# Gated linear attention and an MLP mixer on one core: batch 0's decay logits loaded in runs of four tokens, small work of batch 0 rearranged

## The chip, the cores and the metric

The kernel runs on one core of a Trainium2 chip. The metric is device time in microseconds (us) for one execution. A profiled execution gives a trace; its span is the time from the first to the last instruction, and some time lies around it.

## The reference

Four inputs q, k, v and f_logit, each [4 batches, 8 heads, 768 tokens, 48], float32, and the weights of a mixer. Cut to what is computed:

```python
f = 1.0 / (1.0 + np.exp(-f_logit))
state = np.zeros((B, H, D, D))
for t in range(S):
    state = f[:, :, t, :, None] * state + einsum('bhd,bhe->bhde', k[:, :, t], v[:, :, t])
    y[:, :, t] = einsum('bhd,bhde->bhe', q[:, :, t], state)
x = y.transpose(0, 2, 1, 3).reshape(B, S, 384)
h = np.maximum(x.transpose(0, 2, 1) @ w_tok1, 0.0) @ w_tok2      # tokens: 768 -> 256 -> 768
u = x + h.transpose(0, 2, 1)
out = u + np.maximum(u @ w_ch1, 0.0) @ w_ch2                     # channels: 384 -> 1536 -> 384
```

## The kernel before

A batch's 768 tokens are six chunks of 128, one token to a partition. A decay f becomes L = ln(1 + exp(-f_logit)); the running sum of L inside a chunk is a matmul with a triangle of ones. With G = exp(-sum) and Gi = exp(sum), a chunk is an ordinary masked product: q*G and k*Gi are turned by TensorE, multiplied with each other ("scores"), masked (AmT) and multiplied with v; a 48 x 48 state for each head carries the rest to the next chunk.

For one chunk the steps are, with their lines:

- f, k, q and v are loaded (`load`, L368). f of batch 0 goes through SP's DMA queue, one transfer of 128 x 8 x 48 float32 for each chunk, in runs of 48 floats (192 bytes). k, q and v go through POOL's queue, which casts them to bf16. A `mark` (L364) is a one-element memset by POOL into the place where a chunk's f will land: the transfer on SP waits for it, so it starts when POOL has come so far.
- `gates` (L449): Exp and Ln on ScalarE (L456, L457). L is float32; its upper two bytes are read as a bf16 (`Lhi`), and VectorE subtracts them from L for a second bf16 (`Llo`, L462). For batch 0 this split is made for chunks 0 to 2 only (`SPLIT = 3`).
- `sums_and_turns` (L505): the sums on TensorE. Split chunks take eight one-column matmuls for the sum at the chunk's end (L527, L528) and two of 384 columns with `tri_bf` (L529, L530); chunks 3 to 5 of batch 0 do both in float32 (L518, L520). ScalarE makes G, Gi and `glast` (L540, L542, L545), VectorE multiplies them on q and k (`qk`, L550), TensorE turns them (L560), VectorE or ScalarE copies the result to `qkT`.
- `attention` (L464): scores (L479, on 48 rows from partition 0 or 64) and the chunk's own part of the state (L495).
- `rest` (L578): AmT (L597, or for two halves of batch 0 a copy on ScalarE L589 and a mask on POOL L592), `tsum` and `state` (L606, L609, L611), its copies to `state_bd`, the output matmuls (L628, L635), and copies of the output from PSUM as `x_bf` (bf16) and `x_nat` (float32). For chunks 3 to 5 of batch 0 the output stays in its PSUM bank (`KEPT = 3`), where tok2 adds to it.

`mixer` (L660) then runs tok1 (L665, relu to `h1T`), tok2 (L677), the sum u (L687, and `u_bf`), transposes of u (L699, `uT` L704), ch1 (L715, relu to `zT`, in two halves of the tokens, `th`) and ch2 (L734, final sum L740, store L744).

The order is not written out. Every step is an `Op` with the engines that may do it, a rank, and what it needs and makes. `Plan.order` (L179) places all of them by a table of costs; where it may choose it takes the earliest start, shifted by a lag, and then the lowest rank. `SHIFTS` (L20) replaces rank and lag of 382 numbered steps. The result is a fixed program for each engine, in which every engine works strictly in its order and waits on semaphores. The planner hands out the eight PSUM banks too, and where it expects TensorE to be idle early in the run it puts in matmuls on a constant tile (`idle`, L781, the fills), into bank 7, which is kept for them until 25.5 us of its own clock.

On POOL the order of DMA issues is the order in which `load` and `load_w` are called (L394 to L428): batch 0's chunks, tok1's, tok2's and the two halves of ch1's weights, f and two chunks of batch 1, ch2's weights, and so on. POOL also makes the constants `tri` (a triangle) and `ident` (an identity) at the start.

Of the kernel before, what the change touches and what calls it, by code (L numbers as in the profile page):

```python
# [20 lines left out]
    (5,-30,1300), (13,0,1400), (15,0,800), (46,200,3000), (73,30,1000), (78,90,900), (80,120,900),  # L21
    (90,300,1600), (98,300,1300), (137,30,1100), (141,30,1500), (143,30,1200), (145,60,800), (150,60,800),
    (151,-457,1500), (152,60,800), (154,60,800), (157,60,800), (158,60,1000), (159,60,1100), (161,60,1400),
    (163,60,1800), (164,60,1800), (166,90,1600), (168,90,1000), (170,90,400), (174,90,800), (175,-217,1100),
    (179,90,500), (180,90,800), (182,90,600), (184,90,1400), (186,90,1000), (187,90,2500), (192,120,400),
    (194,120,1600), (195,120,800), (198,120,1600), (210,150,1500), (211,150,1000), (213,150,1100),
    (215,150,1700), (216,150,1400), (218,150,1600), (220,150,1000), (221,150,500), (222,150,800), (224,842,0),
    (225,270,900), (226,270,1600), (229,270,1600), (232,275,200), (233,275,600), (241,281,1500),
    (247,283,2000), (248,283,2700), (250,284,2300), (252,284,2800), (253,285,3000), (255,285,3100),
    (256,290,2500), (258,291,2300), (260,292,2000), (261,292,2600), (263,293,3200), (265,294,3100),  # L30
    (267,295,3000), (269,300,1600), (270,703,400), (271,305,700), (273,310,1900), (274,-287,0), (275,315,2800),
    (276,806,0), (278,-324,0), (279,325,2200), (281,330,700), (283,335,400), (286,457,0), (288,459,0),
    (292,360,200), (294,1119,400), (295,365,1000), (296,370,200), (299,375,100), (300,55,0), (301,380,500),
    (304,390,100), (306,-148,0), (307,395,800), (309,400,300), (310,727,400), (311,405,2100), (312,410,300),
    (313,410,300), (314,415,400), (315,415,2300), (321,267,0), (322,405,0), (324,460,500), (326,540,0),
    (331,540,100), (337,393,0), (341,620,300), (342,633,100), (350,330,100), (355,225,0), (356,410,200),
    (358,490,800), (359,490,900), (360,490,1100), (361,490,1000), (362,490,1200), (365,300,900),
    (366,300,3400), (367,300,1100), (371,370,300), (387,360,700), (389,360,800), (390,360,400), (392,360,2400),
    (393,360,1800), (395,425,0), (397,360,900), (398,346,2400), (399,360,1400), (401,360,1600), (402,360,1300),
    (404,440,900), (407,440,1300), (408,54,0), (410,440,300), (411,490,1000), (414,440,600), (416,440,300),  # L40
    (421,440,400), (425,440,600), (428,440,100), (430,440,300), (431,440,300), (438,440,900), (440,520,600),
    (441,568,800), (442,530,800), (443,520,500), (451,520,400), (458,408,0), (461,520,300), (463,520,700),
    (466,520,300), (471,399,0), (473,380,0), (477,38,0), (478,676,0), (498,584,500), (508,-265,0),
    (510,-105,0), (512,194,0), (513,585,1700), (516,765,0), (520,422,0), (521,711,1400), (524,544,0),
    (525,725,1400), (534,914,0), (535,760,1300), (536,855,0), (538,717,0), (540,843,0), (541,781,1300),
    (544,290,0), (551,816,1700), (552,699,0), (554,528,0), (556,506,0), (558,702,0), (560,1007,0), (562,998,0),
    (569,1029,0), (570,905,1300), (572,1308,0), (573,1122,0), (574,980,600), (577,998,0), (580,995,1800),
    (589,1115,300), (593,590,200), (597,590,1300), (598,467,0), (601,703,0), (602,690,300), (603,690,300),
    (604,790,200), (605,790,600), (607,790,400), (608,790,1100), (615,620,400), (623,727,0), (630,620,900),
    (633,730,0), (634,620,1500), (636,620,600), (637,620,1200), (638,620,1200), (640,620,2700), (642,740,0),  # L50
    (645,720,400), (646,720,200), (647,720,600), (648,730,600), (649,720,1100), (651,720,400), (657,662,0),
    (658,518,0), (667,720,3200), (671,720,700), (672,739,0), (673,720,1400), (674,720,2100), (679,720,1200),
    (680,720,900), (681,854,0), (683,820,400), (685,820,300), (687,820,1600), (691,820,1000), (693,820,400),
    (698,820,1800), (700,820,1600), (701,820,1600), (702,820,3200), (708,820,1200), (715,574,0), (721,631,0),
    (728,970,1700), (731,971,2100), (734,972,1600), (737,973,1600), (739,974,1200), (740,974,3000),
    (743,975,1400), (746,971,600), (751,1222,800), (753,974,400), (754,890,0), (760,1094,200), (762,1101,400),
    (766,1253,0), (770,1179,0), (771,1129,300), (772,275,0), (774,1358,0), (784,1178,700), (785,1178,2500),
# [21 lines left out]
    (1077,1914,4400),  # L79
)  # L80
KEPT = 3
SPLIT = 3


class Op:
# [200 lines left out]
def kernel(  # L286
# [12 lines left out]
    nc = tc.nc  # L299
# [515 lines left out]
```

## Time and profile before

| | us |
|---|---|
| median of 3 runs | 183.9 |
| lowest, highest | 183.29, 185.35 |
| the profiled execution | 183.67 |
| its span | 181.9 |
| mean granted TensorE clock | 0.991 |
| busy: TensorE, VectorE, ScalarE, POOL | 171.4, 128.2, 111.4, 86.1 |
| fills (27 records of 30 instructions) | 9.6, the last at 27.5 |

Fills count as busy time of TensorE. A matmul's record runs from its start to a modelled end, and several are in flight, so the sum of records says less than the distance of starts. The page's slices are 4.55 us long. In a row of a timeline the columns are start, duration of the group, engine, line and operation, output and inputs, count, and in brackets the idle time of the engine just before it and what ended it. In the chain they are start, duration and what. In a table of stretches they are the stretch and its length, then for each engine its busy time and number of instructions, then the granted clock and the DMA figures.

When batch 0's f arrives is read from its six transfers: issued at 0.8, 1.4, 3.3, 7.4, 10.0 and 12.7 us, the first used at 3.42, the second at 5.83, the last four landing 4.4, 4.7, 5.8 and 6.5 us after their issue.

### The profile page before, as it was taken

Reading aid. Unit: us, or ns where it says so; the run is one execution under the profiler, and the core shown is the slowest. Engines: PE = TensorE matmul, PEld = TensorE weight load, DVE = VectorE, ACT = ScalarE, POOL = GpSimd, SP = SyncE. Lnnn points to the kernel's source line nnn. Section 1 sums busy time; section 2 is a strip of 40 time slices with the busy share of each in tenths; the row PEclk is TensorE's granted clock in tenths of the full one; section 3 lists DMA queues with packets and bytes.
Section 4 is the critical chain, followed back from the end, with each engine's and each line's share of the span. In section 5 each row is a group of like instructions: output and inputs, shape, how many; then the busy total and the mean of one; then the engine's idle time right before and its main releaser. Section 6 shows DMA issues by size and latency. Waiting matters only on the chain.

```text
span 181.9 us, 4513 instructions
## 1 busy us (share of the span) xinstructions
PE 171.4 (94%) x1807; PEld 111.7 (61%) x1810; DVE 128.2 (70%) x279; ACT 111.4 (61%) x268; POOL 86.1 (47%) x114
## 2 busy tenths in 40 slices
PE   6759998899999998999999999999999999999992
PEld 2337755566767765676766676776666566666662
DVE  7558996849788986997868849798976736344123
ACT  5558884679995469986789646648754402564100
POOL 7999628947579918979656812221201001000000
PEclk9987999999999999999999999999999999999999
DMA  7999996999999999999999991110000004110033
GB/s 101 131 168 156 140 204 87 228 185 160 197 143 156 273 166 147 97 122 68 225 152 116 128 165 43 44 46 4 0 4 0 2 4 173 43 43 0 4 130 130
DMA packets 88820, 19.95 MB, mean 110 GB/s; under 512 B 81536, under 2 KB 87984, under 8 KB 88800
## 3 DMA queue, kind: packets, MB, share of 16 engines
q0 software_dynamic: 78960, 13.77, 94.8%
q1 hardware_dynamic: 9840, 5.90, 11.1%
q8 instruction: 14, 0.23, 0.5%
q14 instruction: 6, 0.05, 0.1%
HBM read 25.17 MB, written 4.72 MB: 164 GB/s over the span
## 4 chain that ended last, share of the span: by engine, by line
PE 52%; DMA 22%; POOL 12%; ACT 6%; DVE 3%; issue 2%; DVEq 0%; POOLq 0%; ACTq 0%
PE ps L734 19%; PE ps L715 13%; DMA f_sb<-in_f_logit_dram 11%; DMA w_ch<-in_moe_w_ch_dram 8%; POOL qk_sb L379 6%; PE ps L560 3%; PE ps L677 3%; DMA qk_sb<-in_q_dram 3%; POOL v_sb L379 2%; PE ps L665 2%; PE ps L479 2%; POOL f_sb L379 1%; PE ps L518 1%; PE ps L635 1%; PE ps L781 1%
## 5 line engine op out<-in xcount | busy, mean ns | idle before, releaser
L734 PE MATMUL ps<-w_ch,zT 128*128 128x384 bf16 (+2 forms) x300 | 53.0, 319 | 0.0
L715 PE MATMUL ps<-uT,w_ch 128*128 128x384 bf16 x288 | 51.6, 326 | 0.0
L445 ACT ACTIVATE zT<-ps 128x384 bf16<-128x384 f32 x72 | 34.7, 493 | 20.4 <-PE ps L715 19.7
L734 PEld LDWEIGHTS <-zT 128*128 128x128 bf16 x300 | 28.0, 98 | 16.6
L715 PEld LDWEIGHTS <-w_ch 128*128 128x128 bf16 x288 | 27.1, 98 | 16.5
L597 DVE TENSOR_TENSOR AmT<-ps,tri_bf 128x512 bf16<-128x512 f32 x46 | 30.3, 683 | 5.1 <-PE ps L479 4.8
L740 DVE TENSOR_TENSOR x_nat<-x_nat,ps 128x384 f32<-128x384 f32 (+2 forms) x25 | 13.3, 535 | 13.8 <-PE ps L734 13.4
L379 POOL DMA_DIRECT2D qk_sb<-in_q_dram x19 | 18.6, 977 | 4.8 <-DMA w_ch<-in_moe_w_ch_dram 3.1
L379 POOL DMA_DIRECT2D qk_sb<-in_k_dram x19 | 18.8, 987 | 3.8 <-DMA f_sb<-in_f_logit_dram 2.7
L440 POOL CAST state_bd<-state 48x192 bf16<-48x192 f32 x20 | 7.5, 374 | 24.7 <-DVE state L611 11.3
L379 POOL DMA_DIRECT2D v_sb<-in_v_dram x19 | 18.7, 985 | 0.9 <-issue 0.9
L560 PE MATMUL ps<-ident,qk 128*128 128x128 bf16 x192 | 15.3, 221 | 2.4 <-DVE qk L550 2.2
L447 DVE TENSOR_SCALAR zT<-ps 128x384 bf16<-128x384 f32 x24 | 12.7, 552 | 6.8 <-PE ps L715 6.7
L550 DVE TENSOR_TENSOR qk<-qk_sb,GG 128x768 bf16<-128x768 bf16 (+1 forms) x30 | 14.1, 482 | 4.2 <-DMA qk_sb<-in_q_dram 3.1
L560 PEld LDWEIGHTS <-qk 128*128 128x128 bf16 x192 | 12.1, 99 | 6.3 <-DVE qk L550 4.4
L456 ACT ACTIVATE f_sb<-f_sb 128x384 f32<-128x384 f32 x24 | 12.1, 523 | 5.2 <-DMA f_sb<-in_f_logit_dram 5.2
L540 ACT ACTIVATE GG<-ps 128x384 bf16<-128x384 f32 x24 | 11.7, 488 | 5.4 <-PE ps L530 4.9
L462 POOL TENSOR_TENSOR Llo<-L 128x384 bf16<-128x384 f32 x11 | 9.0, 826 | 12.5 <-ACT L L457 12.4
L436 ACT ACTIVATE u_bf<-x_nat 128x384 bf16<-128x384 f32 x17 | 8.1, 521 | 10.7 <-DVE x_nat L687 10.7
L573 DVE COPY qkT<-ps 128x1024 bf16<-128x1024 bf16 x18 | 12.2, 684 | 1.0 <-PE ps L560 0.5
L457 ACT ACTIVATE L<-f_sb 128x384 f32<-128x384 f32 x24 | 12.3, 519 | 0.3
L687 DVE TENSOR_TENSOR x_nat<-x_nat,ps 128x384 f32<-128x384 f32 x21 | 10.4, 549 | 2.9 <-PE ps L677 2.9
(70 smaller groups left out, 256.4 us busy)
## 6 DMA issues: line engine op xcount, KB each, us to landing
out_dram<-x_nat SPq DMA_DIRECT2D x23, 192.0 KB, 1.9
f_sb<-in_f_logit_dram POOLq DMA_DIRECT2D x3, 1152.0 KB, 10.7
qk_sb<-in_k_dram POOLq DMA_DIRECT2D x18, 96.0 KB, 6.8
qk_sb<-in_q_dram POOLq DMA_DIRECT2D x18, 96.0 KB, 6.1
v_sb<-in_v_dram POOLq DMA_DIRECT2D x18, 96.0 KB, 6.1
f_sb<-in_f_logit_dram SPq DMA_DIRECT2D x6, 192.0 KB, 4.6
w_ch<-in_moe_w_ch_dram POOLq DMA_DIRECT2D x2, 576.0 KB, 8.0
w_ch<-in_moe_w_ch_dram POOLq DMA_DIRECT2D x1, 1152.0 KB, 13.9
```

Of the source, the lines that this page charges most:

```text
L379: lambda eng=eng, into=into, of=of: eng.dma_start(out=into, in_=of),
L445: nc.scalar.activation(out_, in_, AF.Relu, bias=0.0, scale=1.0)
L447: nc.vector.tensor_scalar(out_, in_, 0.0, None, ALU.max)
L456: add(ACT, r, lambda: nc.scalar.activation(fb, fb, AF.Exp, bias=0.0, scale=-1.0), make=[key], kind=el)
L457: add(ACT, r, lambda: nc.scalar.activation(full, fb, AF.Ln, bias=1.0, scale=1.0), need=[key], make=[whole], kind=el)
L550: add(DVE, r, lambda n=n: nc.vector.tensor_tensor(qk[i][:, n, :, 0:D], qk_sb[nb][:, n, :, c, :], GG[i][:, n], ALU.mult), need=[(x, nb, c) ...
L560: nc.tensor.transpose(to[:, o + hp, :], blk(src)[:, hp, :], ident)
L573: add(DVE, r, lambda: nc.vector.tensor_copy(qkT[i], banks[p_t[0].at].bitcast(BF16).rearrange("p (n t) -> p n t", t=C)), make=[("qkT", i, 0 ...
L597: add(DVE, r, lambda half=half, made=made: nc.vector.tensor_tensor(half, made(), tb4, ALU.mult), need=["tri_bf"], make=[("AmT", i, p)], ba ...
L715: nc.tensor.matmul(banks[pm.at][:, 0:384], lhsT=w[:, kt, c0:c0 + 128], rhs=uT[:, kt, cols], start=(kt == 0), stop=(kt == 2))
L734: nc.tensor.matmul(banks[pm.at][:, 0:n1 - n0], lhsT=zT[:, kt, tt * 128:(tt + 1) * 128], rhs=w_ch2[:, kt, n0:n1], start=(kt == 0), stop=(kt ...
L740: add(DVE, rank("ch2", tt), lambda un=un, pm=pm, n=n1 - n0: nc.vector.tensor_tensor(un, un, banks[pm.at][:, 0:n], ALU.add), make=[("x_nat" ...
```

## The change

Chunks 2 to 5 of batch 0 (`WIDE`) get their f in two transfers (one for even, one for odd heads) in which partition p holds tokens 4p to 4p+3 of those 512, so that a run is 4 x 48 floats (768 bytes). Both are issued right behind the f of chunks 0 and 1; no mark is left. Exp, Ln and the split are done on half of all this at a time (`wide_gates`). Token 4p+j then lies in row p, part j, and chunk 2+g lies in the row quarter from 32g: its sum is made of matmuls on 32 rows each, for the four parts j, for the upper and the lower bf16 (`wide_sums`). The triangle's rows in that order (`tri4`) are made on TensorE with a picking matrix (`wide_constants`); both borrow space in `zT`. The four chunks' sums leave in four banks at once, the sums at the chunks' ends in one piece (`glast_w`). G and Gi get five buffers instead of two.

```diff
-SPLIT = 3
+WIDE = range(2, 6)
...
+    def load_wide(n):
+        hs = slice(n, H, 2)
+        of = f_logit[0, hs, 2 * C:6 * C].rearrange("h (p j) d -> p h (j d)", j=4)
+        into = f_sb[0][:, hs, 2:6, :].rearrange("p h j d -> p h (j d)")
+        add(SP, -8.0, lambda: nc.sync.dma_start(out=into, in_=of), ...
...
     load("f", 0, 0, SP)
     load("f", 0, 1, SP)
-    load("kq", 0, 0)
-    mark(2)
-    load("f", 0, 2, SP)
-    load("v", 0, 0)
+    load_wide(0)
+    load_wide(1)
+    load("kqv", 0, 0)
...
-    add(POOL, -6.0, lambda: make_identity(nc, ident), make=["ident"], kind=("load", 550, 550, 0))
+              "ident": lambda: nc.vector.tensor_tensor(ident[:, 1:C], tri[:, 1:C], tri[:, 0:C - 1], ALU.subtract),
+              "ident0": lambda: nc.vector.tensor_copy(ident[:, 0:1], tri[:, 0:1])}[x]
     for c in range(1, NCH):
-        load("kq", 0, c)
-        if c + 2 < NCH:
-            mark(c + 2)
-            load("f", 0, c + 2, SP)
-        load("v", 0, c)
+        load("kqv", 0, c)
...
+    def wide_constants():
+        every = ident.rearrange("k (r j) -> k j r", j=4).unsqueeze(2).broadcast_to((128, 4, 4, 32))
+        add(DVE, -4.0, lambda: nc.vector.tensor_copy(pick4.rearrange("k j (g r) -> k j g r", g=4), every), ...
+        def rows():
+            for j in range(4):
+                nc.tensor.matmul(banks[p_m.at][:, j * C:(j + 1) * C], lhsT=pick4[:, j, :], rhs=tri_bf,
+                                 start=True, stop=True)
...
+    def wide_gates(r):
+        for n in range(2):
...
+            add(ACT, r, lambda fb=fb: nc.scalar.activation(fb, fb, AF.Exp, bias=0.0, scale=-1.0), ...
+            add(ACT, r, lambda fb=fb, full=full: nc.scalar.activation(full, fb, AF.Ln, bias=1.0, scale=1.0), ...
+            add(DVE, r, lambda full=full, hi=hi, lo=lo: nc.vector.tensor_tensor(lo, full, hi, ALU.subtract), ...
...
+        def sums():
+            for j in range(4):
+                for part in (hi, lo):
+                    for g in range(4):
+                        rows = slice(32 * g, 32 * g + 32)
+                        nc.tensor.matmul(banks[p_s[g].at][:, 0:DM], lhsT=tri4[rows, j, :], rhs=part[rows, :, j, :, 0:D],
+                                         start=(j == 0 and part is hi), stop=(j == 3 and part is lo))
+        def ends():
+            for hp in range(HP):
+                g4 = banks[p_s[0].at][:, DM + 4 * hp:DM + 4 * hp + 4]
+                for j in range(4):
+                    for part in (hi, lo):
+                        nc.tensor.matmul(g4, lhsT=part[:, hp, j].rearrange("t par d -> t (par d)"), rhs=ones4, ...
...
-                nc.tensor.matmul(pm[:, 0:DM], lhsT=tri, rhs=L[0][:, c, :, 0:D], start=True, stop=True)
-                for hp in range(0 if last else HP):
-                    nc.tensor.matmul(pm[:, DM + hp:DM + hp + 1], lhsT=blk(L[0][:, c])[:, hp, :], rhs=ones,
-                                     start=True, stop=True)
```

The small work: `ident` comes from differences of `tri` on VectorE instead of a mask on POOL; the products with q and k are one instruction from chunk 1 on; `x_bf` of chunks 0 to 2 of batch 0 is copied from `x_nat` (by POOL, ScalarE or VectorE) instead of from PSUM, and that of chunk 5 in two halves; relu of tok1 in batch 0 in two halves, tok2's two matmuls of a tile as two steps; u of chunks 0 to 2 is written as bf16 straight from the sum, and once more as float32; `uT` of batch 0 may be copied by ScalarE; the product with `glast` may go to POOL for batch 0's chunks 3 and 4 and for batches 2 and 3.

```diff
+        else:
+            op = add((POOL, ACT, DVE), r + 10.0, None, need=[xn], make=[xb], kind=("el", DM, False, 1))
+            op.fn = lambda op=op: copy_on(op.engine, x_bf[0][:, c, :], x_nat[0][:, c, :])
...
+            half = DM // 2 if b == 0 else DM
+            for n0 in range(0, DM, half):
...
+            for kts in ((0,), (1,)) if b == 0 else ((0, 1),):
...
+            if b == 0:
+                add(DVE, r, lambda plus=plus, tt=tt: plus(u_bf[:, tt, :]), need=[("x_nat", xn, tt)], ...
+                add(DVE, r + 2.0, lambda plus=plus, un=un: plus(un), make=[("x_nat", xn, tt)], ...
```

`SHIFTS` is replaced as a whole (379 entries; the steps are numbered anew). In the program that comes out, ScalarE's order at the start is Exp and Ln of chunk 0, of chunk 1, the first wide Exp, G and Gi of chunk 0, the first wide Ln, G of chunk 1 and its `glast`, the second wide Exp and Ln, then the rest of chunk 1. TensorE makes the sums of chunks 0 and 1, `tri4`, the transposes of chunk 0, ten fills, scores and state part of chunk 0, then the wide sums and ends, and from there the chunks in turn. Its fills are 30 as before. Of batch 0's mixer it runs ten of the twelve tok2 matmuls, nine transposes, the last two tok2, 18 ch1 matmuls, the other nine transposes and 27 more of ch1. POOL issues the second half of ch1's weights behind one copy of `x_bf` and the two masks. At the end the last tile's 96 columns are done four tiles earlier and its 288 columns last.

## The prediction

> **What bounds the kernel now.** I first read the busy shares and slices of the page.
>
> ```profile
> PE 171.4 (94%) x1807; PEld 111.7 (61%) x1810; DVE 128.2 (70%) x279; ACT 111.4 (61%) x268; POOL 86.1 (47%) x114
> ...
> PE   6759998899999998999999999999999999999992
> ...
> PEclk9987999999999999999999999999999999999999
> DMA  7999996999999999999999991110000004110033
> ```
>
> TensorE has holes only in the first eight slices (4.55 us each). Busy time of pipelined matmuls flatters, so I checked the rest by stretches.
>
> ```profile
> 35.70:60.00 24.30, 24.30 (x276) 16.13 (x274) 19.13 (x41) 19.98 (x53) 17.09 (x19) 1.00 1.96 170
> ...
> sum 142.30, PE 140.95 PEld 93.03 DVE 100.65 ACT 87.10 POOL 57.57; mean PE 20.14 PEld 13.29 DVE 14.38 ACT 12.44 POOL 8.22
> ```
>
> From 35.7 to 178 us TensorE (second number) idles 1.35 us of 142.3. Spaced as the chain shows them (45 matmuls of 384 columns in 7.31 us: 0.163 each), the matmuls left at 35.7 make some 140 us. So the second part is fixed, and the time is where batch 0's ch1 (L715) begins plus that. The change can win before 35.7, and at most 2.3 us behind it. The TensorE timeline shows what ends the first part:
>
> ```profile
> 9.88 0.40 PE L560 MATMUL ps<-ident,qk 128*128 128x128 bf16 x4
> 12.15 0.61 PE L560 MATMUL ps<-ident,qk 128*128 128x128 bf16 x4 [1.88 <-DVE qk L550]
> ...
> 29.61 0.37 PE L635 MATMUL ps<-v_sb,AmT 128*128 128x48 bf16 x8
> 29.82 1.38 PE L665 MATMUL ps<-x_bf,w_tok 128*128 128x384 bf16 x7
> 31.85 2.11 PE L677 MATMUL ps<-h1T,w_tok 128*128 128x384 bf16 x12 [0.65 <-DVE h1T L447]
> 33.80 0.22 PE L699 MATMUL ps<-ident,u_bf 128*128 128x128 bf16 x1
> 34.47 1.44 PE L699 MATMUL ps<-ident,u_bf 128*128 128x128 bf16 x17 [0.45 <-ACT u_bf L436]
> 35.74 7.48 PE L715 MATMUL ps<-uT,w_ch 128*128 128x384 bf16 x45
> ```
>
> Two parts: the six chunks up to the outputs of chunk 5 (E, 29.98), then 5.76 us of small steps to ch1. In the first, VectorE works 14.3 of the 16 us from 12 to 28 and TensorE runs fills; VectorE's and ScalarE's queues set the pace, behind one wait for data, told by the chain:
>
> ```profile
> 6.46 5.25 DMA qk_sb<-in_q_dram
> 11.73 0.37 DVE qk L550
> ```
>
> **The change, up to E.**
>
> *POOL.* The identity mask (0.20 and 0.66) and four marks (0.03 of issue each) leave its queue. Chunk 1's k was issued at 5.57, now at 4.65, and the 15 loads behind it about 1 us earlier at 0.87 apiece. Chunk 1's q lands 5.2 to 7 us after 5.5, at 10.8 to 12.5; it is needed at 14.6 (below), so the old wait is gone from the path. TensorE's identity now costs VectorE 0.3 us in a wait.
>
> *The wide loads.* Two transfers of 384 KB on SP, runs of 768 bytes, right behind f of chunks 0 and 1; the latter landed at 5.8. No row has such a load. From 8.4 to 19.9 us twelve loads of 1024 short runs landed, 0.95 each: by bytes a wide load costs two of these, by runs half of one. With POOL's loads sharing the engines, the first lands at 6.8 to 8.6 and the second at 7.7 to 11.4. At the far end SP keeps only the rate of chunk 1's f (192 KB in 2.4 us, 80 KB per us): 10.6 and 15.4. I take 7.5 and 9; the nearest rows are the loads on the same queue and by bytes weights move faster here (209 GB/s at 24 to 28 us and 230 at 32 to 36, against 139 to 173 from 4 to 20).
>
> *ScalarE.* 384 elements take 0.52 and 128 more 0.11 (0.49 against 0.60 from PSUM), so a wide Exp or Ln of 768 takes 0.85. It works in program order, and chunk 0's two exponentials, which began at 6.8, now stand behind the first wide Exp: Exp 7.5 to 8.35, G and Gi of chunk 0 (0.39 apart) to 9.2, Ln to 9.95, G of chunk 1 and the small one 10.5, second Exp 11.25, Ln 12.15, Gi of chunk 1 12.7. Chunk 0 is thus 1.7 us later than before.
>
> *VectorE.* qk of chunk 0 to 9.55; first Llo (768 elements: 0.55 and 0.40 more by the slope to AmT's 512 at 0.68) 10.95; tri4 11.6; two qkT 12.25; second Llo 12.2 to 13.2.
>
> *TensorE.* Transposes of chunk 0 end at about 9.8, ten fills follow (0.216 each warm: 12.0; partly cold, 13.1), then scores and parts of chunk 0 (0.65), so the wide sums begin at 13.75. Removed for chunks 2 to 5: 0.6 us, three fp32 sums (0.65) and eight fp32 ends (0.10 each), 3.3 together. Added: four matmuls for tri4 (0.25), 32 of a row quarter, 32 small ends (0.026 by L527: 0.84). Scores on half the rows (L479) went out 0.034 apart, full-row transposes of the same 128 columns 0.056, so parts on different rows do overlap: 32 quarters take between 8 x 0.163 = 1.3 (four abreast) and 5.2 (in turn); I take 1.4. Sums and ends finish at 15.15 and 16.0.
>
> The Trainium skill, "TensorE: Matmul & The Clock Gate", section "Part 3: Packing small matmuls", has four row quarters of 512 columns at 3.07 times: by an estimate from that, 1.7 us here, 0.3 more.
>
> *From there VectorE's queue.* Chunk 1's transposes end at 16.45. Then up to the last AmT: 4 qkT (0.35), 4 qk (0.5), 8 AmT (0.61), 8 of tsum and state (0.34), one x_bf (0.35): 11.4 us. x_bf from PSUM and two Llo are gone from it. Without waits it ends at 27.9 and E is 28.3; at the 89% of before it ends at 29.3 and E is 29.7. ScalarE has 12.3 us of its own in that time, and four banks stay held until eight exponentials have run, so I take E = 28.7, a gain of 1.3.
>
> **Behind E.** x_bf of chunk 5 and h1T go in halves on two engines: 0.33 instead of 0.49 and 0.55, about 0.35 in all. The first half of tok2 starts after h1T's first part. Chunks 3 to 5 need only a copy from PSUM, and their transposes and 18 ch1 matmuls no longer wait for the adds of chunks 0 to 2, whose u_bf skips ScalarE. Worked out: tok2 at E+1.2, first u_bf E+2.05, third E+2.95, nine transposes to E+3.45, copies to uT on two engines, ch1 at E+3.95: 1.8 less than 5.76. The second nine transposes come after 18 matmuls with nothing between them and the ch1 that needs them: 0.17, two copies (0.41 and 0.34), 0.55 given back. Net gain 1.25.
>
> What hides the rest: x_bf of chunks 0 to 2 goes to POOL, ScalarE and VectorE from x_nat, due at about 24 and needed at 27; on POOL it waits for x_nat in front of the second w_ch1 load, which was issued at 28.84 behind two masks and two state copies. With the state copies away it goes at about 25.5, with f of batch 1 behind it, so that stream moves by about 3 us too, as much as TensorE. If it moved less, batch 1's Exp on ScalarE would hold up the zT copies queued behind it. The last store is 288 columns instead of 96: 0.2 (1.8 against 1.6 to landing), against one add less at the end (0.25): nothing.
>
> **Sum.** 1.3 + 1.25 = 2.55 off the profiled run of 183.67 (span 181.9 and 1.77 around it) is 181.1. That run lies 0.2 under the median of 183.9; I keep 181.1.
>
> **Rivals.**
>
> *The wide loads are late (0.12), the slower side.* All of chunks 2 to 5 hangs on the second one, and chunk 0 on the first. The gain is used up when the wide sums begin 2.55 later, that is, when the second Exp starts at 13.6 instead of 10.4: landing after 13.6. At 15.4 (80 KB per us) the sums start 4.4 later: 185.5, and 186.5 if VectorE also keeps its 89%. For it: chunk 5's f took 6.5 us under load. Against: that load queued behind far more of POOL's than are out at 3 us.
>
> *The quarters run in turn (0.06).* 3.8 us more: 184.9, or 185.9 with VectorE at 89%. L479 speaks against it.
>
> *Cold clock (0.14).* The row first:
>
> ```profile
> 11.50:12.00 0.50, 0.00 (x0) 1.00 2.58 141
> 12.00:12.50 0.50, 0.35 (x4) 0.57 2.11 179
> 12.50:13.00 0.50, 0.28 (x4) 0.50 1.73 213
> ```
>
> After 1.88 us without matmuls the granted clock fell to 0.50 and came back at 15.5. In the new order TensorE idles from 6.05 to 7.5 and again before the transposes, some 2 us of the stretch to 9. If that halves the clock through fills and sums, fills cost up to 2.1 and sums 1.4 more; part lies beside VectorE's second Llo: about 2 lost, 183.1. The Trainium skill, "TensorE: Matmul & The Clock Gate", section "Part 1: The HAM clock gate", has the clock decided in free-running windows of 3.4 us, an idle one halving it; the 3.3 us of half clock agree, though here 1.88 us of idling was enough, so the measurement decides. By that rule the phase, not the order, says which fill is cold.
>
> *Given back later (0.10).* The static order behind 40 us meets loads or adds at other moments: 1 to 2 us of holes where 1.35 are now, 182.5 to 183.5. For it: the DMA slices are full to 113 us.
>
> *VectorE runs without waits (0.12).* E = 28.3 or better, 0.55 not given back: 179.5 to 180.2.
>
> The forecast keeps 0.46.
>
> **Numbers.** About 1% (1.8 us) is what can be told from no change. Faster: the forecast, the last rival and 0.08 of the clock and later cases: 0.66. Same: the rest of those two (0.16), 0.03 of late loads and 0.03 of the quarters: 0.22. Slower (185.7 and over): the rest of these two, 0.12. The range runs from the best case less half a microsecond for the holes behind 35.7, 179.0, to 184.5, which leaves out the late loads at their far end and the quarters in turn.
>
> **What would show it.** ch1's first matmul near 33.2 instead of 35.74; the first wide Exp at 7.5 and the second at 10.4 without a wait for f; the wide sums 1.4 us long from 13.75; E near 28.7; E to ch1 about 4; and behind ch1 the same 142 us. A second Exp after 12, sums of 5 us, or a clock of 0.5 at 13 to 15 would make it wrong in the way named; ch1 at 33 with an end that has not moved would mean the later rival.

## The result: 3.3% slower, and where the 6 us went

The changed kernel takes 189.77 us (median of 4 runs, 189.14 to 191.32) where the kernel before took 183.59 beside it (183.03 to 185.35): a ratio of 1.033, 95% interval 1.023 to 1.043. Forecast were 181.1, range 179.0 to 184.5. The profiled run took 189.14, its span is 187.4 (before: 183.67 and 181.9). Medians, here and below, are of all runs, while ratios and intervals leave out the runs in a slower state (over 1.5% above the fastest of the same kernel), so a ratio can differ from that of the medians (e3: 1.017 against 1.026).

First the page of the changed kernel: TensorE's totals, its slices (now 4.69 us long), the granted clock and the DMA share.

```profile
PE 173.7 (93%) x1846; PEld 110.9 (59%) x1846; DVE 127.7 (68%) x275; ACT 113.4 (61%) x272; POOL 87.2 (47%) x109
...
PE   6589996999999988999959999999999999999992
...
PEclk9969999999999999999996999999999999999999
DMA  6999999999999995998999990120000102200024
```

The first slices look much as before. New are a 5 in the slice from 94 us and, one slice on, a clock of 0.6. Stretches of 20 us say the same. Before:

```profile
60.00:80.00 20.00, 19.27 (x235) 13.31 (x233) 17.69 (x38) 16.08 (x43) 14.47 (x17) 1.00 1.67 168
80.00:100.00 20.00, 19.67 (x237) 13.11 (x236) 15.67 (x32) 15.47 (x37) 14.87 (x15) 1.00 1.67 134
```

After:

```profile
60.00:80.00 20.00, 18.57 (x274) 12.49 (x271) 18.12 (x37) 15.96 (x45) 14.34 (x17) 1.00 1.53 151
80.00:100.00 20.00, 17.74 (x178) 11.64 (x179) 14.04 (x32) 14.11 (x34) 11.21 (x11) 0.97 1.41 115
```

TensorE (second number) lost 0.7 us in the first of these stretches and 1.9 in the second, which the kernel before did not lose.

**A ruler for the rest.** The order of matmuls differs, so I compare not at the same moment but at the same work left. From the trace I added up, from the end backwards, what the matmuls would take at full clock: 0.015 us and 0.384 ns a column each (0.163 for 384 columns, as they follow each other), float32 times four, a row quarter a quarter, fills nothing. "Arrears" are how much later than the profiled kernel before a kernel has the same work left; below nothing it is ahead. Between neighbouring rows they jump by up to 1 us where the order differs. The ruler's us are some 4% short of real ones: the last 145 of them take 139.5 us in the kernel before.

| us of work left | before, at us | after, at us | arrears |
|---|---|---|---|
| 145 | 38.99 | 38.74 | -0.25 |
| 140 | 43.91 | 43.72 | -0.20 |
| 125 | 57.79 | 58.07 | 0.28 |
| 105 | 77.59 | 78.81 | 1.23 |
| 90 | 91.09 | 93.11 | 2.02 |
| 85 | 96.47 | 101.65 | 5.18 |
| 80 | 100.98 | 106.59 | 5.61 |
| 0 | 178.48 | 183.66 | 5.18 |

So the start gained 0.2 us instead of 2.55, 2.2 us were lost between 44 and 93 us (most of it behind 58), 3.2 between 93 and 102, and from there to the end the kernels run level. Where the large loss will be, the kernel before has these rows of POOL and of ScalarE:

```profile
83.50 2.25 POOL L379 DMA_DIRECT2D f_sb<-in_f_logit_dram  x1
85.71 0.88 POOL L440 CAST state_bd<-state 48x192 bf16<-48x192 f32 x2
```
```profile
93.29 0.52 ACT L456 ACTIVATE f_sb<-f_sb 128x384 f32<-128x384 f32 x1 [0.86 <-DMA f_sb<-in_f_logit_dram]
```

The same places in the changed kernel's timelines of ScalarE, TensorE and POOL:

```profile
92.55 0.49 ACT L456 ACTIVATE zT<-ps 128x384 bf16<-128x384 f32 x1 [0.20 <-PE ps L820]
96.56 0.52 ACT L536 ACTIVATE f_sb<-f_sb 128x384 f32<-128x384 f32 x1 [3.53 <-DMA f_sb<-in_f_logit_dram]
96.99 0.47 ACT L456 ACTIVATE zT<-ps 128x384 bf16<-128x384 f32 x1
```
```profile
93.36 2.12 PE L820 MATMUL ps<-uT,w_ch 128*128 128x384 bf16 x12
97.52 0.65 PE L820 MATMUL ps<-uT,w_ch 128*128 128x384 bf16 x3 [2.04 <-ACT zT L456]
```
```profile
81.98 0.34 POOL L451 CAST state_bd<-state 48x192 bf16<-48x192 f32 x1 [1.63 <-PE ps L820]
82.30 0.82 POOL L540 TENSOR_TENSOR Llo<-L 128x384 bf16<-128x384 f32 x1
83.47 0.54 POOL L451 CAST state_bd<-state 48x192 bf16<-48x192 f32 x1 [0.36 <-DVE state L688]
84.21 0.92 POOL L383 DMA_DIRECT2D qk_sb<-in_q_dram  x1 [0.20 <-issue]
85.11 0.88 POOL L383 DMA_DIRECT2D v_sb<-in_v_dram  x1
85.98 2.24 POOL L383 DMA_DIRECT2D f_sb<-in_f_logit_dram  x1
```

Read upwards from the end: POOL issues batch 3's f at 85.98 (before: 83.50), because q, v and that f now stand behind two copies of `state_bd` that wait for batch 2, where before f stood ahead of such copies. f lands at 96.54 (before: 93.27). ScalarE came to the Exp of this f at 93.0 and waits 3.53 us, with relu copies to zT behind it in its fixed order; TensorE's ch1 needs the PSUM banks that those copies free, and stands still for 2.04 us. Before, the same Exp waited 0.86 us. What follows is read in stretches (busy time of TensorE first, the granted clock third from the end):

```profile
95.50:97.50 2.00, 0.00 (x0) 0.00 (x0) 1.13 (x3) 0.94 (x3) 0.60 (x1) 1.00 2.78 145
97.50:98.60 1.10, 1.08 (x10) 0.74 (x10) 0.00 (x0) 1.10 (x4) 1.10 (x1) 1.00 3.90 110
98.60:102.00 3.40, 3.40 (x24) 2.05 (x21) 1.32 (x3) 2.42 (x7) 2.78 (x6) 0.50 1.63 83
102.00:104.00 2.00, 2.00 (x34) 1.48 (x31) 0.85 (x2) 1.42 (x4) 2.00 (x1) 0.99 2.73 145
```

1.1 us after the hole the clock is halved for 3.4 us, at most 1.7 us more. TensorE is "busy" all through it, so busy time alone would not show this part.

### The profile page after: what moved, and what is told of

Same layout as the page of the kernel before. It is cut to its first block, busy times and chain, and to the rows that moved or that the text cites. A ratio compares the mean times of both kernels' runs of the same rounds, so it can differ in the third digit from the quotient of the medians.

```text
span 187.4 us, 4579 instructions
## 1 busy us (share of the span) xinstructions
PE 173.7 (93%) x1846; PEld 110.9 (59%) x1846; DVE 127.7 (68%) x275; ACT 113.4 (61%) x272; POOL 87.2 (47%) x109
## 4 chain that ended last, share of the span: by engine, by line
PE 52%; DMA 21%; POOL 10%; DVE 7%; ACT 4%; issue 3%; DVEq 0%; POOLq 0%; ACTq 0%
PE ps L839 19%; PE ps L820 13%; DMA qk_sb<-in_q_dram 8%; DMA w_ch<-in_moe_w_ch_dram 7%; DMA f_sb<-in_f_logit_dram 6%; POOL qk_sb L383 4%; PE ps L633 3%; PE ps L768 3%; PE ps L752 2%; PE ps L892 2%; POOL f_sb L383 2%; POOL v_sb L383 2%; DVE AmT L670 2%; PE ps L557 2%; PE ps L712 1%
## 5 line engine op out<-in xcount | busy, mean ns | idle before, releaser
L839 PE MATMUL ps<-w_ch,zT 128*128 128x384 bf16 (+2 forms) x300 | 54.2, 325 | 0.0
L820 PE MATMUL ps<-uT,w_ch 128*128 128x384 bf16 x288 | 50.4, 326 | 2.1 <-ACT zT L456 2.0
L456 ACT ACTIVATE zT<-ps 128x384 bf16<-128x384 f32 x71 | 34.1, 490 | 11.0 <-PE ps L820 10.7
L458 DVE TENSOR_SCALAR zT<-ps 128x384 bf16<-128x384 f32 x25 | 13.2, 552 | 9.3 <-PE ps L820 9.3
L451 POOL CAST state_bd<-state 48x192 bf16<-48x192 f32 x15 | 5.8, 387 | 27.8 <-DVE state L688 18.4
L447 ACT ACTIVATE state_bd<-state 48x192 bf16<-48x192 f32 x25 | 9.0, 361 | 12.2 <-DVE state L681 5.2
L752 PE MATMUL ps<-x_bf,w_tok 128*128 128x384 bf16 x48 | 12.9, 325 | 1.0 <-DVE x_bf L449 0.8
L536 ACT ACTIVATE f_sb<-f_sb 128x384 f32<-128x384 f32 x20 | 10.0, 521 | 5.7 <-DMA f_sb<-in_f_logit_dram 5.7
L447 ACT ACTIVATE x_nat<-ps 128x384 f32<-128x384 f32 x19 | 9.0, 503 | 6.9 <-PE ps L712 6.9
L540 POOL TENSOR_TENSOR Llo<-L 128x384 bf16<-128x384 f32 x12 | 10.0, 849 | 4.8 <-ACT L L537 4.7
```

Of the source, the lines that this page charges most:

```text
L447: nc.scalar.activation(out_, in_, AF.Copy, bias=0.0, scale=1.0)
L456: nc.scalar.activation(out_, in_, AF.Relu, bias=0.0, scale=1.0)
L458: nc.vector.tensor_scalar(out_, in_, 0.0, None, ALU.max)
L752: add(PE, rank("tok1", rt), lambda rt=rt, kt=kt, pm=pm: nc.tensor.matmul(banks[pm.at][:, 0:DM], lhsT=w_tok1[:, kt, rt * 128:(rt + 1) * 128 ...
L820: nc.tensor.matmul(banks[pm.at][:, 0:384], lhsT=w[:, kt, c0:c0 + 128], rhs=uT[:, kt, cols], start=(kt == 0), stop=(kt == 2))
L839: nc.tensor.matmul(banks[pm.at][:, 0:n1 - n0], lhsT=zT[:, kt, tt * 128:(tt + 1) * 128], rhs=w_ch2[:, kt, n0:n1], start=(kt == 0), stop=(kt ...
```

## The experiments

All keep the computation whole. Most only move steps: the planned order is a list, and a step n is taken out and put ahead of a step m, which moves it on its engine's queue alone. The edit has this form, and only its pairs are shown from then on:

```diff
-    for op in plan.best(idle, 6500.0, 25500.0):
+    seq = list(plan.best(idle, 6500.0, 25500.0))
+    for n, m in ((837, 838), (849, 850)):
+        op = plan.ops[n]
+        seq.remove(op)
+        seq.insert(seq.index(plan.ops[m]), op)
+    for op in seq:
         op.fn()
```

Times, with the ratio to the kernel before in runs beside them on the same chip, and the arrears of the profiled run. "Late half clock" is a stretch of 0.5 behind 40 us.

| run | median us | before | ratio, 95% | arrears at 140, 90, 80, 0 us left | late half clock |
|---|---|---|---|---|---|
| e1_exp_later | 189.38 | 184.94 | 1.022 (1.013 to 1.031) | 0.8, 3.0, 6.6, 6.2 | 102.8 to 106.2 |
| e2_loads_first | 189.63 | 184.94 | 1.027 (1.017 to 1.036) | 0.5, 2.7, 5.1, 4.6 | none |
| e3_both | 189.69 | 184.94 | 1.017 (1.004 to 1.030) | 1.2, 3.6, 5.9, 5.4 | none |
| e4_few_fills | 187.27 | 184.94 | 1.010 (1.001 to 1.020) | -0.8, 2.4, 4.7, 4.3 | none |
| after_again | 190.02 | 185.35 | 1.030 (1.023 to 1.038) | -0.2, 2.1, 6.2, 5.8 | 98.6 to 102.0 |
| e5_before_f_late | 192.02 | 185.35 | 1.042 (1.033 to 1.051) | 0.0, 0.3, 6.5, 6.6 | 100.8 to 104.2 |
| e6_f_early | 186.39 | 185.35 | 1.010 (1.001 to 1.020) | 1.3, 4.6, 4.3, 3.9 | none |
| e7_wide_gated | 191.74 | 185.35 | 1.040 (1.032 to 1.048) | 2.2, 4.5, 8.0, 7.6 | 101.0 to 104.4 |
| e8_f_early_few_fills | 186.66 | 184.30 | 1.011 (1.006 to 1.015) | -1.2, 2.4, 2.2, 1.8 | none |
| e9_gate_f_early | 187.55 | 184.30 | 1.018 (1.011 to 1.024) | 0.7, 4.4, 4.2, 3.7 | none |
| e10_exp_and_q_later | 186.05 | 184.30 | 1.010 (1.007 to 1.013) | 0.6, 2.8, 2.6, 2.1 | none |
| e11_e10_few_fills | 184.44 | 184.37 | 1.002 (0.998 to 1.005) | -1.1, 0.8, 0.6, 0.1 | none |

The granted clock of the first 14 to 22 us differs from run to run of one kernel, so arrears at 140 us tell less than what is added behind.

**e1: the Exps out of the way on ScalarE.** Steps 837 and 849 are the first two Exps of batch 3, 838 and 850 their Lns, behind the zT copies (the edit above).

> The changed kernel with two steps moved on ScalarE: the first two Exps of batch 3 stand just ahead of their Lns, behind the zT copies that were queued behind them. Theory A (the held queue): ScalarE waited 3.5 us at 93.0 for f of batch 3 with zT copies behind it, TensorE lost 2.0 us waiting and some 1.7 us more at half clock from 98.7 to 102.1; both go, so 3 to 4 us less than the changed kernel, about 185.5 to 186.5, and no half clock behind 20 us. Theory B (batch 3's data themselves are late): batch 3's sums wait for f anyway, the hole moves to about 110 us and less than 1 us is gained.

The hole at 95 us is gone, and TensorE has a new one of the same size 4.6 us later. Its timeline, then POOL's:

```profile
102.10 0.33 PE L705 MATMUL ps<-state_bd,qkT 128*128 128x96 bf16 x4 [2.03 <-POOL state_bd L451]
```
```profile
98.48 2.21 POOL L383 DMA_DIRECT2D qk_sb<-in_q_dram  x1 [7.05 <-ACT GG L615]
100.75 0.50 POOL L688 TENSOR_TENSOR state<-tsum,glast 128x192 f32<-128x192 f32 x1
101.32 0.72 POOL L451 CAST state_bd<-state 48x192 bf16<-48x192 f32 x2
```

POOL waits 7.05 us to issue q of batch 3, and behind q stand the state steps that TensorE needs. The releaser named, G on ScalarE, is only the event that came last by the profile: q was issued 0.36 or 0.37 us after f had landed here (98.11) and in the profiles of before (93.27), after (96.54), e5 (98.41) and e6 (91.69). So the late f blocks a second queue; what that issue waits for besides (the expectation of e10 calls it room) the record does not show. The expectation that the hole simply closes fell: with arrears of 6.2 at the end nothing was gained, as Theory B had it, though by another way than its late sums.

**e2 and e3: the loads of batch 2 ahead of the five Llo on POOL**, without and with e1's moves.

```diff
+    for n, m in ((98, 600), (99, 600), (100, 600)):
```

> The changed kernel with three loads (k, q, v of batch 2's chunk 3) moved on POOL ahead of the five subtractions (Llo of batch 2) for which POOL waited from 67 to 74 us. Theory A: the loads fill POOL's wait, f of batch 3 is issued near 83.5 instead of 86.0 and lands 2.5 us earlier, the hole at 95 us goes mostly and with it the half clock: 2.5 to 4 us less than the changed kernel, unless the first sums of batch 2, whose Llo come up to 1 us later, take some of it back. Theory B (the time lies in the holes from 66 to 81 us, not in the load): no gain or a loss of up to 1 us.

> Both moves. Theory A: the two take away the same hole, so not the sum of them: 3 to 5 us less than the changed kernel, 185 to 186. What is left over the kernel before (1.5 to 2.5 us) then lies in the holes from 66 to 81 us. Theory B: as the better of the two alone.

The five Llo were not what made f late. POOL then waited 4.26 us at the `state_bd` copy instead of 1.63, and issued f at 86.64 (e2) and 87.57 (e3). TensorE's holes stayed: 2.46 us on zT in e2, 2.33 on `state_bd` in e3. By the arrears at the end, 4.6 and 5.4, neither gained the 2.5 to 5 us of Theory A.

**e4: four fills instead of ten** behind chunk 0's transposes.

```diff
-        for _ in range(n):
+        for _ in range(4 if n == 10 else n):
```

> The changed kernel with the run of ten fills ahead of chunk 0's scores cut to four. In the trace the ten took 3.5 us at half clock and ended at 14.3, 1.9 us after qkT. Theory A: the wide sums start 1 to 1.5 us earlier, ch1 near 33.7 instead of 34.9, but the end does not move by more than 0.5 us, since POOL's stream and the wait for f of batch 3 stand where they were. Rival C (the start sets the end): the whole kernel is 1 to 1.5 us faster. If TensorE stays at half clock for want of fills, the sums take 2.8 instead of 1.4 us and nothing is gained at the start either.

The changed kernel's timeline of TensorE, then that of e4:

```profile
10.02 1.04 PE L633 MATMUL ps<-ident,qk 128*128 128x128 bf16 x8 [1.85 <-DVE qk L623]
10.85 3.53 PE L892 MATMUL ps<-steady 128*128 128x512 bf16 x10
14.31 0.40 PE L557 MATMUL ps<-qkT 48*128 48x128 bf16 x8
```
```profile
11.02 1.91 PE L892 MATMUL ps<-steady 128*128 128x512 bf16 x4
12.87 0.61 PE L557 MATMUL ps<-qkT 48*128 48x128 bf16 x8
```

The ten fills held back the scores that were ready at 12.4, when VectorE's copies to qkT ended. In e4 the sums start at 13.75 instead of 14.88 and ch1 at 34.30 instead of 34.87; at 140 us of work left the gain is 0.6 us beyond the changed kernel's. By 90 us left it is gone (arrears of 2.4 against 2.0). The end comes 0.9 us earlier, but the hole behind 95 us, 2.38 us here, stays without a half clock this time, which alone was worth up to 1.7 us. So e4 leaves open whether a start that gains carries through; e11 below answers it.

**after_again and e5: the suspected cause alone, put into the kernel before.** Steps 364 and 365 of that kernel are the loads of f and k of batch 3.

```diff
+    for n, m in ((364, 365),):
```

> The changed kernel as it is, beside the three others on the same chip, so that each of them is compared with it directly. All theories: 3 to 4% slower than the kernel before, as in the first result.

> The kernel before with one change: POOL issues batch 3's f (L379, 83.5 us in its profile) three state_bd copies later, at about 87 us. Theory A (the largest loss of the changed kernel, 3.2 us between 93 and 102 us, comes from batch 3's f being issued 2.5 us later, which holds ScalarE's first Exp of batch 3 with zT copies behind it, and then halves TensorE's clock): f lands at 96.5 to 98 us instead of 93.3, the first Exp of batch 3 waits 4 to 5 us instead of 0.86, TensorE stands idle for 1 to 2.5 us between 95 and 101 us, and the kernel before becomes 2 to 5 us slower. Theory B (the loss is spread over the new order of all engines; this load is only one late thing among many, with slack behind it): at most 1 us slower.

The changed kernel repeats its arrears within 0.1 us up to 90 us of work left. In the kernel before, one load moved behind three copies costs 6.7 us in the median, more than the whole change does and more than the 2 to 5 that Theory A had. Its POOL, ScalarE and TensorE:

```profile
87.70 0.35 POOL L440 CAST state_bd<-state 48x192 bf16<-48x192 f32 x1 [0.78 <-DVE state L611]
88.00 2.23 POOL L379 DMA_DIRECT2D f_sb<-in_f_logit_dram  x1
```
```profile
98.43 0.52 ACT L456 ACTIVATE f_sb<-f_sb 128x384 f32<-128x384 f32 x1 [5.67 <-DMA f_sb<-in_f_logit_dram]
```
```profile
99.77 0.65 PE L715 MATMUL ps<-uT,w_ch 128*128 128x384 bf16 x3 [4.18 <-ACT GG L542]
101.21 1.04 PE L560 MATMUL ps<-ident,qk 128*128 128x128 bf16 x8 [0.79 <-DVE qk L550]
```

f was issued 4.5 us later than before and landed 5.1 later. Up to 90 us of work left this kernel is 0.3 us behind, 10 us of work later 6.5: 4.97 of waiting and the half clock. Nothing else of the change is in it. The wait that the profile of before shows at this place was 0.86 us and looked harmless.

**e6: f early in the changed kernel.** e2's three loads, and q (105), v (106) and f (367) ahead of the `state_bd` copy 634.

```diff
+    for n, m in ((98, 600), (99, 600), (100, 600), (105, 634), (106, 634), (367, 634)):
```

> The changed kernel with two changes on POOL: k, q and v of batch 2's chunk 3 are issued before the five Llo of batch 2, and q and v of its chunk 5 and the f of batch 3 before the state_bd copies behind which they stood. The f of batch 3 is issued at about 80.5 us instead of 85.98. Theory A (above): it lands near 91 us, the first Exp of batch 3 no longer waits at 93 us, neither the wait of 2 us on zT nor the half clock at 98 to 102 us appears; TensorE's arrears against the kernel before at 85 us of work left are 1 to 2.5 us instead of 5.2, and the time is 3 to 4 us below the changed kernel. Theory B, by what moving the Exps alone did: the hole moves to another place again, at most 1 us is gained. Theory C (DMA is the limit there): f issued earlier takes longer to land, and the Exp still waits over 2 us.

f is issued at 81.95 and lands at 91.69; neither the hole nor the late half clock is there, and the time is 3.6 us below the changed kernel's. Arrears added behind 140 us of work left are 2.6 instead of 5.4 to 6.0. A new wait of 0.55 us on Llo at 73.6 us came with the loads ahead of the Llo.

**e7: the start rearranged.** A one-element memset by POOL behind the issue of chunk 0's q holds the wide loads back to 3.4 us; ScalarE's and VectorE's steps are moved as the expectation says, and four fills.

```diff
+    for n, m in ((3, 7), (4, 7), (73, 74), (110, 76), (130, 76), (121, 82), (122, 82), (120, 82), (75, 82), (78, 82)):
...
+    gate = Op((POOL,), 0.0, lambda: nc.gpsimd.memset(f_sb[0][0:1, 0:1, 2:3, 0:1], 0.0), (), (), None, ("fix", 90, 90))
+    seq.insert(seq.index(plan.ops[3]), gate)
```

> The changed kernel with its start rearranged: POOL sets one element of the place of the wide f behind the issue of chunk 0's q, so that both wide loads start at about 3.4 us instead of 1.9; ScalarE's first wide Exp stands behind G and Gi of chunk 0, Gi of chunk 1 ahead of the second; VectorE's two wide Llo behind chunk 0's AmT; the ten fills behind chunk 0's transposes are four. Theory A (the start gained only 0.25 us of work because the wide loads hold back chunk 0's q, which landed at 9.5 us instead of 7.05, and because ten fills ran at the lower clock): q lands at 7 to 7.5 us, the transposes of chunk 0 start at 7.6 to 8.2 instead of 10.02, ch1 starts 1 to 2 us earlier than 34.87, and the end follows by 0.5 to 2 us. Theory B (what is late is the wide sums themselves): ch1 starts within 0.5 us of 34.87 or later, as the wide f lands 1.5 us later.

q landed at 8.30 instead of 9.50, the transposes started at 8.81, and the start was 2.4 us later all the same. TensorE and VectorE:

```profile
12.34 0.35 PE L505 MATMUL ps<-L,zT 32*128 32x384 bf16 x4
15.47 0.38 PE L505 MATMUL ps<-Llo,zT 32*128 32x384 bf16 x4 [2.78 <-DVE Llo L491]
```
```profile
13.01 0.68 DVE L670 TENSOR_TENSOR AmT<-ps,tri_bf 128x512 bf16<-128x512 f32 x1
13.60 1.82 DVE L491 TENSOR_TENSOR Llo<-L 128x768 bf16<-128x768 f32 x2
```

The wide sums waited for Llo, which I had put behind a product that itself waits for the scores. That is a fault of this experiment, so it tells little of the gate.

**e8, e9 and e10: two ways to mend both places.** e8 issues f early but moves only one load ahead of the Llo, with four fills; e9 is e8 with the gate, the Llo where they end first, and two fills; e10 leaves f late and takes out of its way what stood behind it on both queues (369 is the load of batch 3's q, 848 the Llo behind the state steps).

```diff
+    # e8; e9 has besides (3, 7), (4, 7), (73, 74), (81, 75), (115, 75), (116, 75) and the gate
+    for n, m in ((98, 600), (105, 634), (106, 634), (367, 634)):
...
+    # e10
+    for n, m in ((837, 838), (849, 850), (369, 848)):
```

> The changed kernel with batch 3's f issued early on POOL (ahead of the state_bd copies, and of batch 2's chunk 3 only k ahead of the five Llo, so that TensorE's new wait of 0.55 us on Llo at 73.6 us goes) and with four fills instead of ten behind chunk 0's transposes. Theory A (late f, and fills at the lower clock, each cost what their own runs showed: 3.6 us and about 2 us): 184 to 185.5 us where the kernel before takes 184 to 185.5, the same within 1%; arrears of TensorE against the kernel before 1.5 to 3 us from 90 us of work left to the end if both start at the same clock. Rival (the two gains are not independent, an earlier start meets the same loads and waits longer for them): 186 us or more.

> The same with two fills there, and with both wide loads behind the issue of chunk 0's q again, but this time VectorE's two wide Llo stand where they end first (behind chunk 0's copies to qkT, ahead of its AmT), and ScalarE's first wide Exp behind G and Gi of chunk 0. Theory A (the gate itself helps, as q landed 1.2 us earlier with it; what cost the time in the first gated run was my placing of the two Llo behind AmT, for which TensorE waited 2.78 us in the wide sums): the wide sums start without a wait at 13.0 to 13.8 us instead of 14.88, ch1 starts at 33 to 34.3, and the time is 0 to 1 us below the run above. Theory B (all of the early data together is what the DMA engines can bring by 10 us, so that an earlier q is a later f): wide sums no earlier than in the run above, same time within 0.5 us.

> The changed kernel, f as late as it is there, but with what stands in line behind it moved out of the way on both queues: on ScalarE the two Exps of batch 3 behind the zT copies (as in the first of these experiments), and on POOL the load of batch 3's q, which waits for room, behind the product with glast and the two state_bd copies that stood behind it. Theory A (a late f costs only through what is queued behind its users; with Exp alone moved, TensorE's hole of 2.0 us came back as a wait for state_bd, which stood behind that load): neither hole appears, no half clock behind 90 us, arrears at the end 2 to 4 us instead of 5.2 to 5.9, the time 2 to 3.5 us below the changed kernel. Theory B (f itself is needed by then, whatever the order): a hole of 1.5 us or more comes back between 98 and 112 us at another place, less than 1 us gained.

e8 came out at 186.66, above its 184 to 185.5 and on its rival's side, though by another way than the rival had it. f is in time (landed 90.05), but its issue takes POOL 2.2 us ahead of a `state_bd` copy. In order POOL, VectorE, ScalarE and TensorE of e8:

```profile
80.12 2.29 POOL L383 DMA_DIRECT2D f_sb<-in_f_logit_dram  x1
82.34 0.42 POOL L451 CAST state_bd<-state 48x192 bf16<-48x192 f32 x1
```
```profile
82.79 0.98 DVE L688 TENSOR_TENSOR state<-tsum,glast 128x192 f32<-128x192 f32 x1 [1.15 <-POOL state_bd L451]
```
```profile
83.80 0.36 ACT L447 ACTIVATE state_bd<-state 48x192 bf16<-48x192 f32 x1 [1.81 <-DVE state L688]
84.07 1.22 ACT L456 ACTIVATE zT<-ps 128x384 bf16<-128x384 f32 x3
```
```profile
84.59 0.65 PE L820 MATMUL ps<-uT,w_ch 128*128 128x384 bf16 x3 [1.14 <-ACT zT L456]
```

The copy is late, VectorE's next state waits for it, ScalarE's copy for that state, the zT copies stand behind, and TensorE waits for them: the same kind of chain, 10 us earlier. e9 was 0.9 us slower than e8. Its sums started at 12.52, earlier than hoped, but ran in a half clock that lasted up to 21.3 us in the profiled run, where e8's sums ran at full speed, and ch1 began at 35.79 instead of 33 to 34.3; so whether the gate by itself helps stays open.

e10 did what was expected of it. With f landing at 97.29, later than in the changed kernel, there is neither hole nor half clock:

```profile
80.00:100.00 20.00, 19.74 (x234) 13.26 (x228) 16.45 (x36) 15.88 (x38) 11.91 (x13) 1.00 1.51 119
100.00:120.00 20.00, 19.97 (x208) 13.05 (x205) 14.64 (x30) 11.99 (x29) 8.95 (x11) 1.00 1.26 104
```

So f was not needed by then. What cost the time were the zT copies and the state steps that stood in line behind those who waited for it.

**e11: e10 with four fills**, and a `state_bd` copy ahead of an x_bf copy (428, 432).

```diff
+    for n, m in ((837, 838), (849, 850), (369, 848), (428, 432)):
```

> The run before this one (f late, but the two Exps of batch 3 behind the zT copies and the load of batch 3's q behind the state_bd copies) with four fills instead of ten behind chunk 0's transposes, and with one state_bd copy of batch 1 ahead of an x_bf copy on ScalarE (TensorE waited 0.37 us for it at 67 us). Theory A (the start's fills and the two queues are independent losses): 1 to 1.8 us below the run before, that is 184 to 185.2 us where the kernel before takes 184.3: the same within 1%, TensorE's arrears at the end 0 to 1.2 us. It does not clearly beat the kernel before, since the arrears of 2 us that grow between 57 and 93 us stay but for the 0.37. Rival (an earlier start meets the same loads): 185.5 us or more.

184.44 against 184.37: the loss is gone, and the change then neither gains nor loses. The profiled run is 1.1 us ahead at 140 us of work left and level at the end. Against e10 it is 1.7 us ahead at 140 and 2.0 at 90 and at the end, of which the moved copy can be 0.37: here a gain at the start did carry through. What e11 loses behind 140 is part of the loss between 44 and 93 us. In the changed kernel four waits of TensorE are in that stretch, 1.4 us together (0.37 on a `state_bd` copy behind an x_bf copy, 0.16 on qkT, 0.74 and 0.15 on AmT); only the first was tried, and it went. The rest of that loss was not taken apart. No version tried beats both kernels.

## Why the prediction was wrong, step by step

*"So the second part is fixed, and the time is where batch 0's ch1 (L715) begins plus that."* This step failed, and it decides. From ch1's first matmul to the last of the kernel it took 142.7 us before and takes 148.8 now (34.87 to 183.66). The page of before showed TensorE without holes there, and I took that for a pace of TensorE's own. It was the pace of an order in which the loads were just in time: the one wait for batch 3's f was 0.86 us, and e5 shows what 4.5 us more on that one load do. The new table rearranges all engines up to the end, and nothing in my working looked at POOL's and ScalarE's order behind 40 us.

*The rival "given back later".* It was the right case, with 0.10, and its price of 1 to 2 us of holes was mis-sized: 2.2 us and then 3.2, of which one hole is 2.04 and the half clock up to 1.7. I had even named the mechanism, for batch 1: "batch 1's Exp on ScalarE would hold up the zT copies queued behind it". Batch 1's f came 1.85 us earlier (issued 27.78) and did no harm. It was batch 3's.

*E = 28.7.* It was about 30.3, 0.3 later than before instead of 1.3 earlier. Most steps up to the sums held: chunk 1's k was issued at 4.68 (4.65 forecast), the wide Exps began at 7.52 and 10.17 (7.5, 10.4), the second Llo ended at 13.23 (13.2). Row quarters went out nearly four abreast: 32 of them in 1.44 us (1.4 taken, 1.7 by the prediction's other estimate, 1.3 if fully abreast), the ends in 0.82 (0.84). But the sums began at 14.88 instead of 13.75. The working had no term for what the wide loads do to the loads of POOL's queue: chunk 0's q landed at 9.50 instead of 7.05 (e7's gate brought it back to 8.30), and its transposes then ran at half clock, so that the fills began at 10.85 and not at 9.8; the ten fills took 3.46 us, most of it at 0.50 of the clock, near the cold price that I had counted, and held the scores 1.9 us past their data (with four, e4's sums began at 13.75). From the end of chunk 1's transposes to E it took 12.6 us against 12.25: VectorE's pace was right.

*Behind E.* 4.6 us to ch1 against 3.95 worked out:

```profile
29.95 0.36 PE L712 MATMUL ps<-v_sb,AmT 128*128 128x48 bf16 x8
31.12 0.48 PE L752 MATMUL ps<-x_bf,w_tok 128*128 128x384 bf16 x2 [0.81 <-DVE x_bf L449]
32.26 1.78 PE L768 MATMUL ps<-h1T,w_tok 128*128 128x384 bf16 x10 [0.65 <-DVE h1T L458]
...
34.87 1.42 PE L820 MATMUL ps<-uT,w_ch 128*128 128x384 bf16 x7
```

ch1 starts at 34.87, 0.87 us earlier than before and 1.7 later than the 33.2 forecast (E + 3.95 is 32.65; the 33.2 has the 0.55 given back in it, which comes behind ch1's start). With half of the transposes still to do, the gain is 0.25 us of work.

*Cold clock.* The half clock came as that rival had it, through the fills, but the sums at 14.88 ran at full speed. (In the kernel before it had lasted 3.41 us, 12.07 to 15.49, and not the 3.3 read there.) That it could come a second time at 98 us was in no case.

## What to carry to other kernels

When every engine runs a fixed order, a busy engine is no proof that it is the bound. Before counting a stretch as fixed, list for each large load who waits for it and what stands behind that waiter on its queue; a wait of under 1 us there can be the edge of a loss of 6. Put a wait for a load behind the copies that the busiest engine needs, on every queue that it blocks (here ScalarE and POOL), and mend both at once: ScalarE's alone only moved the hole (e1); POOL's alone was not tried. Issuing the load earlier works too, as long as its issue (2.2 us on POOL here) does not delay such a copy in turn (e8).

## What the chip showed that I had not expected

*The clock goes by a grid of time, not by the length of the hole alone.* Where both ends can be read from the granted clock in narrow stretches, half clock lasted 3.41 us, 6.83 or 13.65. Behind 40 us, holes of 2.04 and 2.58 us (the changed kernel's two profiles), 2.03 (e1) and 2.01 (e7) brought it on; holes of 2.46 (e2), 2.33 (e3) and 2.38 (e4) did not. Counted in steps of 3.413 us from the end of each run's last half clock before the hole, the first four holes lie whole in one step, at whose end the clock falls; the others lie across a border, with 1.0 and 1.4, 0.8 and 1.5, 1.2 and 1.2 us on its sides. e5's hole of 4.18 us lies across a border too: 1.79 us of it in one step did not bring it on, 2.4 in the next, with more idle time behind, did. So between these long matmuls 2.0 us idle in one step was enough and 1.8 was not. At the start idle time alone does not decide: 1.0 us in a step was enough in e10 (4.54 to 7.96), 1.1 was not in e5 (5.21 to 8.62). The Trainium skill, "TensorE: Matmul & The Clock Gate", section "Part 1: The HAM clock gate", has free-running windows of 3413 ns; the trace agrees. Its table halves the clock after an idle window of about 3.4 us; here 2.0 us within one was enough, so the measurement decides.

*A clock of 1.00 at the very start is no reading.* The record of the granted clock begins where the clock first rises (5.25 us in the profile of before, 6.45 in the changed kernel's, 14.05 in e1's). The first eight fills of both kernels, from 1.5 us on, take 0.61 to 0.63 us each, as fills in half clock later do (0.38 at full clock), though a stretch there reads 1.00. Where the grid lies changes from run to run: at the start the recorded half clock lasted 3.41 us in both profiles of the changed kernel and 6.83 in e6 and e10, whose order there is the same. The time goes with the mean of the recorded clock: 52 of the 54 runs of the kernel before beside these experiments took 182.7 to 184.4 us at 0.998 and over (11 runs), 183.4 to 185.8 at 0.991 (28), 185.3 to 186.2 at 0.981 (7), 186.8 to 187.7 at 0.972 (6).

*Batch 3's f takes about 10 us to land, whenever it is issued*: from 80.12 to 90.05 (e8), 81.95 to 91.69 (e6), 83.50 to 93.27 (before), 85.98 to 96.54 (after), 88.00 to 98.41 (e5). Batch 1's takes longer, 29.63 to 40.55 (before) and 27.78 to 40.00 (after). An issue that is late by one copy's wait is late by all of it at the landing.

*Two loads on SP's queue held back loads on POOL's.* With the wide f issued at 1.91 and 2.59 us, chunk 0's q, issued at 2.39 (before: 2.37), landed at 9.50 instead of 7.05. From 4 to 8 us the trace has packets of 756 KB on SP's queue and 137 KB on POOL's, where before there are 216 and 343. With the wide loads held back to 3.4 us (e7) q landed at 8.30, so about half of the delay is shown to be theirs by a run. The Trainium skill, "DMA: Bandwidth & Descriptors", section "Issuing engines are not separate DMA queues", says that all queues run on the same 16 engines and interleave; the trace agrees.
